# A new order for every engine's list in a two-branch kernel: warming matmuls, PSUM pairs and queues

## The chip, the cores and the metric

The kernel runs on one core of a Trainium2 chip. The metric is the device time of one execution in microseconds (us). TensorE is called PE here, VectorE DVE, ScalarE ACT, GpSimd POOL and SyncE SP, as the profile does. PE writes its results to PSUM, eight banks which this kernel uses as four pairs; ACT (and in four places DVE) takes them from there into SBUF, which is called an eviction. DMA transfers are issued from the queues of SP, ACT and POOL.

## The reference

Two branches work on the same input `x = A_q` (2048 rows, 640 columns) and are mixed by a gate per row.

```python
def _A_ref(q, k, v, shift_k, ssm_k, ssm_D):
    # k_shift: a causal convolution of k with 4 taps per column
    kv = k_shift * v
    # y: a long causal convolution of kv with ssm_k, by FFT of length 2 S
    y = y + kv * ssm_D
    return q * y

def _B_ref(x, w1, w2, w3, w4):
    h = _gelu(_layernorm(x) @ w1)
    # four groups of 160 columns of h, moved by +1, -1, +2, -2 rows
    hs = jnp.concatenate([g0, g1, g2, g3], axis=-1) @ w2
    x1 = x + hs
    return x1 + _gelu(_layernorm(x1) @ w3) @ w4

g = _sigmoid((x * gate_w).sum(-1, keepdims=True))
return g * a + (1 - g) * b
```

## The kernel before, in words

A row number is split as row = 1024 c + 8 p + rho: c is 0 or 1, p is one of the 128 partitions and rho one of 0 to 7. A step on a pair of rho is one of four stages sc.

**Branch B.** DVE takes the statistics of each rho (`bn`, L776 and L778; those of rho 1 are made on ACT, `st`), POOL raises the variance to the power -1/2 (`ln`, L756; this one instruction is called a power below), DVE normalizes (`xn`, L554), PE transposes through PSUM (`xTp`, L821, ten transpositions for one rho; rho 6 and 7 go by DMA, `xTd`, L818) and ACT evicts (`xTe`, L580). Then come the first matmul (`mm1`, L861, with Gelu in the eviction; for rho 0 and 1 in two halves `0a` and `0b`). The last 32 columns of each group come out in a matmul of their own (`gelu1t` is its eviction) and are moved to their places by small DMAs on POOL's queue (`tail`, L901). The second matmul (`mm2`, L971) starts from PSUM pairs that ACT has filled with x (`seed2`, L953). ACT makes the sums and the squares of the second normalization (`x1`, `sq`), and DVE and POOL finish it (`ln`, L794, L800 and L756), ACT normalizes rho 2 to 7 (`xn`, L566), SP transposes by DMA (`xT`, L998), and `mm3` (L1062) and `mm4` (L1033) follow.

**Branch A.** DVE forms kv from the four taps (`kv`, `kvb`, L549). The long convolution is done as a transform by matmuls with cosines and sines (`fwd`, L1091: `fwdh` for the taps of ssm_k, `fwdk` for kv), products on DVE with some of the sums done by accumulating DMAs on POOL's queue (`bh`, `bk`, `pw`, `fold`, L549 and L1121), and an inverse transform (`inv`, L1234). The taps reach SBUF by transpositions on PE for the first 320 columns (`tap`, L711), and by DMA for the others. POOL adds ssm_D to one row of the taps (`ssmD`, L721); the four `fwdh` jobs of the residue that holds this row wait for that.

**What sets the order.** The program first makes a list of 981 nodes (one engine's operation, a block of matmuls, or a DMA) with all their dependences. The class `Prog` then takes two lists that are written out in the source: `RANK` has a number for each node, and each engine works its nodes off in falling order of it; `PAIR` names the PSUM pair of each job of PE. A job waits until the evictions of the last job on its pair are done. `schedule` sorts and adds these dependences, `assign_waits` leaves out the waits that others already imply, and `emit` writes the engines' instruction streams. There is no other planning: an engine whose next node is not ready stands still. The numbers say nothing of times.

**Warming matmuls.** 96 nodes `fill` (L645) are matmuls of ones by ones, 128 columns wide, whose result nobody reads. They stand in `RANK` like the others; those that come behind PE's last useful node are dropped.

```python
    for i in range(FILL):
        P.stage = i * 8 // FILL
        P.pe([(lambda e, ps: e.matmul(bank(ps, 0, 128), ones, ones, start=True, stop=True)) for _ in range(FILLN)], r=[ones],
             cols=128 * FILLN, tag="fill", bits=(False, None))
```

Other small work ahead of and between the first transpositions: `gwt` (L651, five matmuls of one column), `shk` (L656, four times two matmuls that spread the taps over the partitions), `gsum` (L909), `halo` (L667), `gate` (L918).

Of the kernel before, what the change touches and what calls it, by code (L numbers as in the profile page):

```python
# [292 lines left out]
def _bf16_bits(a):  # L293
# [34 lines left out]
R4M = {("h",1),("k",1)}  # L328
FILL = 96
RANK = [  # L330
# [46 lines left out]
]  # L377
PAIR = [
# [7 lines left out]
]  # L386

def _freq(kap):
# [962 lines left out]
```

## Time and profile before

| what | before |
|---|---|
| time, three runs | 222.86, 223.73, 224.98 us; median 223.73 |
| the profiled execution | 226.48 us, span 224.4 us |
| PE busy | 216.7 us, 1520 matmuls, 81 of them warming ones |
| DVE, ACT, POOL busy | 205.3, 171.3, 62.0 us |
| mean granted clock of PE | 0.985 |
| moved by DMA | 39.76 MB |

The span runs from the first to the last instruction of the profiled execution; 226.48 - 224.4 = 2.1 us lie around it. A row of the timeline reads: start, length, engine and line, shapes, number of instructions, and in brackets the idle time ahead of it and who ended it. Matmuls overlap: the length of a row includes the time in which the last one leaves the array, so that the pace is read from one start to the next.

### The profile page before, as it was taken

To read this page: it belongs to the slowest core of one execution; us is meant where nothing else is said; L and a number is where in the kernel's file an instruction comes from. 1 tells how busy PE (TensorE), PEld (TensorE's weight loads), DVE (VectorE), ACT (ScalarE), POOL (GpSimd) and SP (SyncE) were. 2 spreads that over 40 slices of the span, in tenths; PEclk is the share of its full clock that TensorE was granted. 3 is DMA by queue.
4 is the path that set the end of the run, shared out by engine and by line. 5 is a ranking of instruction groups with operands and counts; after the bars stand their busy time and mean duration, and the time that the engine had idled before them with its cause. 6 is when DMAs were issued, how large, how long until landed. Compare 5 with 4: busy or idle time off the path is not lost.

```text
span 224.4 us, 3910 instructions
## 1 busy us (share of the span) xinstructions
PE 216.7 (97%) x1520; PEld 136.3 (61%) x1520; DVE 205.3 (91%) x307; ACT 171.3 (76%) x291; POOL 62.0 (28%) x64
## 2 busy tenths in 40 slices
PE   7899999799999999999999999999999999999993
PEld 7567766545767655446774554457764477666772
DVE  3896999999997999999998999999999989998764
ACT  4767998779999999999999998666423565396480
POOL 1232439255101302190062110222332303237000
PEclk9859999999999999999999999999999999999999
DMA  7999986759965640995443191087997975779768
GB/s 203 365 401 395 403 339 138 191 100 171 304 164 172 226 88 0 317 183 187 94 84 62 27 164 17 0 117 142 182 225 125 225 160 93 141 178 141 110 197 259
DMA packets 41579, 39.76 MB, mean 177 GB/s; under 512 B 20452, under 2 KB 34791, under 8 KB 41432
## 3 DMA queue, kind: packets, MB, share of 16 engines
q1 hardware_dynamic: 33864, 24.75, 38.3%
q0 software_dynamic: 7408, 14.42, 32.0%
q10 hardware_dynamic: 288, 0.33, 0.5%
q8 instruction: 12, 0.20, 0.4%
q14 instruction: 7, 0.06, 0.1%
HBM read 21.60 MB, written 3.93 MB: 114 GB/s over the span
## 4 chain that ended last, share of the span: by engine, by line
PE 66%; ACT 25%; POOL 3%; DMA 2%; DVE 1%; SPq 1%; issue 0%
PE PS L1033 23%; PE PS L1062 16%; ACT arena L580 16%; PE PS L861 8%; PE PS L1234 7%; PE PS L1091 6%; ACT arena L566 5%; ACT PS L953 4%; DMA arena<-in_A_q_dram 2%; POOL arena L901 2%; PE PS L821 2%; PE PS L711 1%; POOL arena L721 1%; PE PS L656 1%; PE PS L667 1%; SPq L592 1%
## 5 line engine op out<-in xcount | busy, mean ns | idle before, releaser
L549 DVE TENSOR_TENSOR arena<-arena 128x1280 bf16<-128x1280 bf16 (+5 forms) x212 | 182.3, 923 | 6.8 <-ACT arena L580 4.6
L580 ACT ACTIVATE arena<-PS 128x640 bf16<-128x640 f32 (+7 forms) x140 | 104.8, 814 | 22.9 <-PE PS L1062 8.0
L1033 PE MATMUL PS<-arena 128*128 128x320 bf16 x384 | 54.4, 299 | 0.5 <-ACT arena L580 0.5
L1062 PE MATMUL PS<-arena 128*128 128x512 bf16 x240 | 54.3, 379 | 0.0
L1033 PEld LDWEIGHTS PS<-arena 128*128 128x128 bf16 x384 | 37.5, 98 | 15.5 <-issue 0.8
L1121 POOL DMA_DIRECT2D arena<-arena x24 | 24.0, 1107 | 71.1 <-DVE arena L549 66.5
L580 ACT ACTIVATE arena<-PS,arena 128x320 bf16<-128x320 f32 (+1 forms) x48 | 26.5, 603 | 21.2 <-PE PS L1033 15.2
L1062 PEld LDWEIGHTS PS<-arena 128*128 128x128 bf16 x240 | 23.0, 98 | 26.8 <-ACT arena L580 1.2
L1091 PE MATMUL PS<-arena 128*128 128x320 bf16 x208 | 33.3, 300 | 1.7 <-POOL arena L721 1.3
L566 ACT ACTIVATE arena<-arena 128x640 bf16<-128x640 bf16 (+2 forms) x34 | 28.5, 865 | 2.0 <-DMA arena<-in_A_q_dram 1.8
L1091 PEld LDWEIGHTS PS<-arena 128*128 128x128 bf16 x208 | 19.0, 98 | 12.9 <-ACT arena L580 3.0
L756 POOL TENSOR_TENSOR arena<-arena 128x4 f32<-128x4 f32 (+1 forms) x9 | 18.7, 2077 | 27.4 <-DVE arena L554 23.9
L861 PE MATMUL PS<-arena 128*128 128x512 bf16 (+1 forms) x125 | 24.4, 353 | 0.0
L953 ACT ACTIVATE PS<-arena 128x640 f32<-128x640 bf16 x32 | 23.5, 744 | 0.3
L971 PE MATMUL PS<-arena 128*128 128x320 bf16 x160 | 22.9, 299 | 0.0
L971 PEld LDWEIGHTS PS<-arena 128*128 128x128 bf16 x160 | 15.2, 98 | 6.8 <-ACT PS L953 0.6
L861 PEld LDWEIGHTS PS<-arena 128*128 128x128 bf16 x125 | 12.7, 104 | 9.6 <-issue 0.5
L1234 PE MATMUL PS<-arena 128*128 128x320 bf16 x112 | 17.0, 299 | 0.0
L776 DVE BATCH_NORM_STATS2 arena<-arena 128x6 f32<-128x320 bf16 x28 | 12.1, 477 | 3.4 <-DMA arena<-in_A_q_dram 3.4
L901 POOL DMA_DIRECT2D arena<-arena x18 | 9.7, 544 | 16.2 <-ACT arena L580 16.2
L1234 PEld LDWEIGHTS PS<-arena 128*128 128x128 bf16 x112 | 10.7, 98 | 5.1 <-ACT arena L580 0.4
L645 PE MATMUL PS<-arena 128*128 128x128 bf16 x81 | 10.5, 277 | 1.2 <-DVE arena L602 1.2
(39 smaller groups left out, 72.8 us busy)
## 6 DMA issues: line engine op xcount, KB each, us to landing
arena<-arena POOLq DMA_DIRECT2D x18, 320.0 KB, 4.6
arena<-in_B_w_dram POOLq DMA_DIRECT2D x4, 960.0 KB, 6.3
arena<-in_A_k_dram SPq DMA_DIRECT2D x4, 640.0 KB, 9.7
arena<-in_A_v_dram SPq DMA_DIRECT2D x4, 640.0 KB, 16.4
arena<-arena POOLq DMA_DIRECT2D x4, 640.0 KB, 6.1
arena<-in_A_q_dram SPq DMA_DIRECT2D x4, 640.0 KB, 7.3
out_dram<-arena SPq DMA_DIRECT2D x15, 160.0 KB, 2.1
arena<-in_A_q_dram SPq DMA_DIRECT2D x6, 320.0 KB, 5.5
```

What stands on the lines that cost most here:

```text
L549: return dve(lambda e: e.tensor_tensor(o, a, b, op), [a, b], [o], c_tt(n), tag=tag, **kw)
L566: node = P.op("act", lambda e, ps: e.activation(o, i, func, **kw), r=r, w=[o], cost=c_act(n, naps, acc is not None, psum=False), tag=tag, ...
L580: node = P.op("act", lambda e, ps: e.activation(ov, inner(ps), func, **kw), r=r, w=[o], cost=c_act(n, len(r), acc is not None), job=job, t ...
L756: P.op("pool", lambda e, ps: e.tensor_tensor(r, v, hv, ALU.pow), r=[v, HALF], w=[r], cost=cost, tag="ln")
L861: fns.append(lambda e, ps, b=b, c=c, lhsT=lhsT: e.matmul(bank(ps, b, 256 * n), lhsT, XT[:, c, r0:r0 + n, :], start=(c == 0), stop=(c == 4)))
L953: P.seed(job, lambda e, ps: e.activation(two(ps, 320), x, ACTF.Copy), [X[:, c, rho, :]], c_act(640, psum=False), tag)
L971: fns.append(lambda e, ps, hh=hh, ft=ft, lhsT=lhsT: e.matmul(bank(ps, hh, 320), lhsT, w2v[:, ft, 320 * hh:320 * hh + 320], start=False, st ...
L1033: fns.append(lambda e, ps, hh=hh, ft=ft, lhsT=lhsT: e.matmul(bank(ps, hh, 320), lhsT, w4h[ft // 6][:, ft % 6, 320 * hh:320 * hh + 320], st ...
L1062: fns.append(lambda e, ps, b=b, ft=ft, c=c, sc=sc: e.matmul(bank(ps, b, 512), w3h[ft // 6][:, c, 128 * (ft % 6):128 * (ft % 6) + 128], XT[ ...
L1091: fns.append(lambda e, ps, w=w, b=b, rhs=rhs, st=(first and n == 0), en=(n == len(ss) - 1): e.matmul(bank(ps, b, 320), w, rhs, start=st, s ...
L1121: return P.dma("pool", lambda e, ps: e.dma_start(o, i, accum_op=ALU.add, max_dma_last_dim=2560), r=[o, i], w=[o], nbytes=nb, cost=1.2, kin ...
L1234: fns.append(lambda e, ps, w=w, z=z, c=c, st=(n == 0), en=(n == len(terms) - 1): e.matmul(bank(ps, c, 320), w, z[:, c, :], start=st, stop=en))
```

## The change

`RANK` and `PAIR` get other numbers; nothing else in the source is touched. No operation is added, removed or changed in size, but for the warming matmuls: 94 of the 96 are now ahead of PE's last useful node, where 81 were.

```diff
 FILL = 96
 RANK = [
-    977, 925, 973, 972, 980, 975, 962, 957, 952, 938, 933, 915, 926, 976, 940, 967, 834, 881, 849, 946, 827,
...
+    978, 977, 965, 972, 980, 964, 959, 949, 954, 924, 907, 916, 877, 973, 930, 971, 802, 873, 793, 936, 783,
...
 PAIR = [
-    1, 0, 2, 2, 3, 1, 2, 2, 1, 1, 3, 1, 1, 1, 1, 3, 2, 3, 0, 3, 0, 3, 3, 1, 0, 0, 1, 2, 0, 2, 1, 1, 3, 2, 2, 3,
...
+    0, 3, 0, 1, 0, 1, 0, 3, 2, 1, 3, 3, 2, 0, 2, 1, 0, 2, 2, 1, 3, 3, 3, 2, 1, 0, 0, 2, 2, 0, 0, 3, 1, 1, 0, 0,
...
```

The numbers can be read only once the nodes are sorted by them. These are the stretches of the lists where the two orders differ most (the number behind a name is the rho or the stage; `fill x24` is 24 warming matmuls).

```
PE before   fill x24, gwt, fill x26, shk, fill x4, gsum, fill x6, xTp:0, shk, fill x2, shk, halo:1, halo:0,
            xTp:1, mm1:0a, mm1:0a, shk, mm1:0b, mm1:0a, mm1:0b, xTp:2, fill, xTp:3, mm1:0b, tap x3, mm1:1, ...
            behind xTp:0 21 more fill: two, then ones, and once five in a row
PE after    fill x63, shk, fill x27, gwt, fill, xTp:0, fill x2, shk, fill, gsum, shk, halo:1, xTp:1, mm1:0a,
            mm1:0a, shk, mm1:0b, xTp:3, halo:0, mm1:0b, xTp:2, tap, mm1:0a, xTp:4, mm1:1, mm1:0b, tap, ...
            behind xTp:0 3 more fill
POOL before ident, ln:0, ln:1, w1t, ln:2, tail:0, ln:4, ln:6, tail x8, ssmD, tail x7, w3:0, tail x2, ssmD,
            w3:1, ln (stage 0), w4:1, w4:0, pwTa, pwSa, GM, ln, ln, ln (stages 1 to 3), pwTa, pwSa, ...
POOL after  ident, ln:0, ln:1, ln:2, w1t, tail x2, ln:4, tail, ln:6, tail x6, ssmD, tail x9, ssmD, w3:0, w3:1,
            ln (stage 0), GM, w4:1, w4:0, ln (stage 1), pwTa, pwSa, ln, ln (stages 2, 3), pwTa, pwSa, ...
SP before   gate_w, x:1, shift_k, x:1, x:3 x2, k:1, w1, x:5 x2, x:7 x2, ssm x3, k:0, D x2, FM:0, w2 x2, v:0,
            FM:1, v:3, v:2, k:3, v:1, kh, w2 x3, xTd x4, w2, k:2, w2 x2, tT ...
SP after    D, shift_k, x:1 x2, x:3 x2, gate_w, k:1, w1, x:5, x:7, x:5, w2, ssm, x:7, k:0, ssm, FM:1, w2 x2, ssm,
            w2, kh, w2 x3, FM:0, v:0, v:2, k:3, v:1, w2, xTd x4, D, k:2, v:3, tT ...
```

On DVE the first normalization `xn:0` moves ahead of a statistics block that waits for the second column block's load, and between the statistics `ln:4` and `xn:4` stand five `bn` operations, where two `xn` and five `bn` stood. ACT's list has the eviction of `gwt` ahead of the first `shk` in both orders, while on PE `gwt` now comes 27 warming matmuls behind that `shk`. On ACT two of the four `xn:5` move ahead of the second `seed4`, and one square of stage 3 moves behind them. PE's last eighteen blocks, from the job ahead of the first `inv` of the second half, have the same pattern in both orders.

102 rows, old and new, of tables (PAIR, RANK) are left out of this document.

## The prediction

> **What bounds the kernel now.** I read the page first, then the chain of waits, then busy times by stretches, and last the timelines of the head.
>
> ```profile
> span 224.4 us, 3910 instructions
> PE 216.7 (97%) x1520; PEld 136.3 (61%) x1520; DVE 205.3 (91%) x307; ACT 171.3 (76%) x291; POOL 62.0 (28%) x64
> PEclk9859999999999999999999999999999999999999
> PE 66%; ACT 25%; POOL 3%; DMA 2%; DVE 1%; SPq 1%; issue 0%
> ```
>
> PE is busy for 97% and carries 66% of the chain that ended last, and DVE with 91% has nearly as little room. The fourth digit of the clock row is a 5: early on the clock was halved for a slice. Two lines of the chain of waits and two stretches (busy PE, PEld, DVE, ACT, POOL, then the clock) tell the rest:
>
> ```profile
> 53.34 1.04 ACT arena L580
> 101.89 6.68 PE PS L1033 x48
> 53.00:101.00 48.00, 47.78 (x346) 29.42 (x345) 45.48 (x59) 47.54 (x103) 13.94 (x13) 1.00 0.67 178
> 101.00:221.00 120.00, 119.01 (x764) 73.48 (x761) 112.97 (x163) 82.21 (x128) 27.76 (x24) 1.00 0.66 130
> ```
>
> From 53.3 to 101.9 us the chain runs over ACT's evictions, and PE is busy for 47.78 of 48 us beside it; from there to the end it is PE alone, 119.01 of 120 us. Behind 53 us an order of the lists can win little: PE's idle time there is 0.2 + 1.0 us, DVE's 2.5 + 7. What can be won lies ahead of 53 us. What can be lost lies anywhere, since three engines are nearly full.
>
> **The clock in the head.** First the clock by half microseconds (the clock is the column ahead of the last two), then PE's timeline.
>
> ```profile
> 9.50:10.00 0.50, 0.50 (x6) 0.12 (x3) 0.50 (x2) 0.27 (x1) 0.00 (x0) 1.00 1.08 381
> 10.00:10.50 0.50, 0.50 (x4) 0.13 (x2) 0.47 (x4) 0.50 (x1) 0.08 (x1) 0.51 1.03 384
> 16.50:17.00 0.50, 0.50 (x5) 0.39 (x4) 0.50 (x3) 0.50 (x2) 0.00 (x0) 0.67 0.96 385
> 1.18 2.74 PE L645 MATMUL PS<-arena 128*128 128x128 bf16 x24 [1.18 <-DVE arena L602]
> 4.07 2.81 PE L645 MATMUL PS<-arena 128*128 128x128 bf16 x26
> 6.81 0.72 PE L656 MATMUL PS<-arena 1*128 1x320 bf16 x2
> 7.83 0.49 PE L645 MATMUL PS<-arena 128*128 128x128 bf16 x6
> 8.97 0.72 PE L821 MATMUL PS<-arena 128*128 128x128 bf16 x10 [0.65 <-DVE arena L778]
> 11.26 1.78 PE L667 MATMUL PS<-arena 128*128 128x480 bf16 x4
> 12.83 1.27 PE L821 MATMUL PS<-arena 128*128 128x128 bf16 x10
> 13.90 3.78 PE L861 MATMUL PS<-arena 128*128 128x256 bf16 x20
> 17.61 0.72 PE L656 MATMUL PS<-arena 1*128 1x320 bf16 x2
> 18.27 2.36 PE L861 MATMUL PS<-arena 128*128 128x256 bf16 x20
> 20.46 0.72 PE L821 MATMUL PS<-arena 128*128 128x128 bf16 x10
> 21.02 0.22 PE L645 MATMUL PS<-arena 128*128 128x128 bf16 x1
> ```
>
> The clock is 1.00 up to 10.0 us, 0.50 from there to 16.7. The warming matmuls show that it was also low at the start, which the page does not record: the 26 of the second row take (6.81 - 4.07) / 26 = 0.105 us each, the six of 7.83 only (0.49 - 0.22) / 5 = 0.054. So PE is slow until about 6.6 us, then fast, then slow again from 10.0 to 16.7. What the second slow stretch costs is read from equal work at full clock: twenty matmuls of 256 columns take 17.61 - 13.90 = 3.71 us in it and 20.46 - 18.27 = 2.19 behind it (1.52 lost); ten transpositions 13.90 - 12.83 = 1.07 against 21.02 - 20.46 = 0.56 (0.51 lost); four of 480 columns 1.57, at half that 0.78 lost. Together 2.8 us, all on PE's path.
>
> Between 6.8 and 10.0 us PE has little dense work: ten warming matmuls, single-row jobs, ten transpositions and 0.65 us of idle time. The new order has 63 + 27 + 1 = 91 warming matmuls ahead of the first transposition, where 24 + 26 + 4 + 6 = 60 stood, and they run on without a hole to the transposition. I take it that the clock then holds: PE's thin stretch shrinks to the time between the first transposition and the first mm1, some 3.3 us with a halo job in it, against 6.8 to 13.9 before. Gain 2.8, bounds 0 and 2.8.
>
> The Trainium skill ("TensorE: Matmul & The Clock Gate", the table "Why this matters for your kernels") asks only for no idle gaps of more than about 3 us. By that rule the 0.65 us could not have halved the clock, the warming matmuls would buy nothing, and the sum would be 2.8 us poorer. The rows disagree: the clock fell at 10.0 us with no gap of that size.
>
> **What the warming matmuls cost.** Fifty run at the slow pace up to 6.8 us, or 6.6 without the gwt job among them. The other 40 ahead of gwt take 40 x 0.054 = 2.2, the shk pair 18.27 - 17.61 = 0.66, gwt about 0.2: the first transposition starts at 9.7 instead of 8.97, 0.75 later. Its input is there by then (it was the wait that ended at 8.97, and xn:0 moves up on DVE). Bounds: nothing if the clock rises a microsecond sooner, 1.3 if it rises so much later. Behind the first transposition 3 warming matmuls stand instead of 81 - 60 = 21: 18 x 0.054 = 1.0 less, of which gsum, which moves behind it, takes 0.1 back: -0.9. Where these stood in waits they cost nothing, so the gain is 0 to 0.9; I keep 0.9, as PE's idle rows are few.
>
> **POOL's small transfers.**
>
> ```profile
> 29.29 3.40 PE L861 MATMUL PS<-arena 128*128 128x512 bf16 x15
> 20.26 0.61 POOL L901 DMA_DIRECT2D arena<-arena  x1 [5.62 <-ACT arena L580]
> 20.90 1.04 POOL L756 TENSOR_TENSOR arena<-arena 128x4 f32<-128x4 f32 x1
> 32.99 4.28 POOL L901 DMA_DIRECT2D arena<-arena  x8 [3.68 <-ACT arena L580]
> 37.29 3.11 POOL L721 TENSOR_TENSOR arena<-arena 1x320 bf16<-1x320 bf16 x1
> 38.53 0.64 PE L918 MATMUL PS<-arena 128*128 128x1 bf16 x20
> 40.46 3.16 PE L1091 MATMUL PS<-arena 128*128 128x320 bf16 x22 [1.29 <-POOL arena L721]
> ```
>
> Eight transfers, held by an eviction of ACT (gelu1t of the second row pair), and the addition of ssm_D behind them keep PE idle for 1.29 us. The new list leaves six between the power ln:6 and the addition: 2 x 4.28 / 8 = 1.1 less. Against that, the five matmuls whose eviction they wait for now follow both blocks of ten of their stage, one block (2.2 us) later than before. ACT has the same evictions ahead of it in both lists. PE being 2.8 - 0.75 = 2.0 ahead, its five (the first of the 15 in the first row, at 0.216 each: 29.29 + 1.1 = 30.4 before) end at 30.4 - 2.0 + 2.2 = 30.6, the eviction by some 31.4 (32.7 before, when ACT came to it late), the transfers by 31.7 + 3.2 = 34.9, the addition by 38.0. Counted at the paces of the rows, PE's list has 27.2 us of work from the first transposition to the waiting job, where 26.85 stood, so PE comes to it at 39.17 - 2.0 + 0.35 = 37.5. The wait shrinks from 1.3 to 0.5: -0.8, bounds -1.3 and +1 (an addition is 3.11 or, by the page's mean of two, less).
>
> **DVE and the end.**
>
> ```profile
> 22.05 0.80 DVE L554 TENSOR_SCALAR arena<-arena 128x640 bf16<-128x640 bf16 x2 [1.86 <-POOL arena L756]
> 71.06 0.16 DVE L794 SCALAR_TENSOR_TENSOR arena<-arena 128x4 f32<-128x4 f32 x1 [1.52 <-ACT arena L580]
> 197.83 4.01 DVE L549 TENSOR_TENSOR arena<-arena 128x1280 bf16<-128x1280 bf16 x5
> 202.63 1.25 PE L1234 MATMUL PS<-arena 128*128 128x320 bf16 x8
> ```
>
> The last fold ends at 201.84 and PE's first inverse job of the second half starts at 202.63: if DVE came no sooner, PE could gain only 0.8 us. So DVE must give some 2.7 to 3 too. Its 1.86 wait is for the power of 20.90, which had stood behind the transfer of 20.26 since that waited 5.62 us for ACT. In the new order two transfers stand ahead of the power, but ACT evicts both halves of gelu1t early; with PE's earlier mm1 they go by 17 to 18 us and the power is there in time. The 1.52 wait is for ACT's squares and shrinks with ACT. Together up to 3.4 us, bounds 0.5 and 3.4. SP's queue costs nothing: k:2 and v:3 now stand behind the four transpositions xTd, but the tap transpositions behind them wait for all loads in both orders, and the product with v:3 comes only behind the row of 71.06; gate_w is needed only by a gwt that is later.
>
> **The sum.** On PE: -2.8 + 0.75 - 0.9 - 0.8 = -3.75; DVE allows -0.8 - 3.4 = -4.2 at best. The other moves (pairs, evictions, products) I take at nothing, bounds -1 and +1 by the 1.2 us of idle time that PE has behind 53. I take -3.5: span 220.9, and the profiled execution 226.48 - 3.5 = 223.0. The median of the runs stands 2.75 below the profiled execution, and the runs differ by 2.1 us. Part of this may be the clock stretch, which a run need not have in full. I count half of it, 1.4, as missing in the median: 223.73 - (3.5 - 1.4) = 221.6, with 220.4 to 222.8 as this case's own range.
>
> **The rivals.** The median has the clock stretch in full: 223.73 - 3.5 = 220.2. For it: the thin stretch from 6.8 to 13.9 us is in every run.
>
> The median does not have it at all: 223.73 - (3.5 - 2.8) = 223.0. For it: the 2.75 us between profile and median are the 2.8 of the clock; against it: the three runs spread over 2.1. The Trainium skill (the same page, Part 1) says that the activity window runs free of the kernel's start, so that such a stretch may fall differently from run to run; no run here shows the clock without a profile.
>
> The clock falls in the new order too, in the thin stretch from 9.7 to 13 us, and halves mm1 and the transpositions as in the rows above: 221.6 + 2.8 = 224.4 at worst. DVE does not come sooner and the end stays where it is but for 0.8: 223.73 - 0.8 = 222.9. Then the change doesn't do on DVE what it does on PE.
>
> Slower: ACT stands still at the first xn:5, which now stands ahead of the second seed4 and the evictions of the transforms.
>
> ```profile
> L953 ACT ACTIVATE PS<-arena 128x640 f32<-128x640 bf16 x32 | 23.5, 744 | 0.3
> 103.34 2.77 ACT L566 ACTIVATE arena<-arena 128x640 bf16<-128x640 bf16 x3
> 99.36 0.16 DVE L800 SCALAR_TENSOR_TENSOR arena<-arena 128x4 f32<-128x4 f32 x1
> 96.58 2.75 POOL L756 TENSOR_TENSOR arena<-arena 128x4 f32<-128x4 f32 x1
> 113.94 5.12 POOL L756 TENSOR_TENSOR arena<-arena 128x4 f32<-128x4 f32 x1 [12.54 <-DVE arena L554]
> ```
>
> Its input is ready at 99.5, 0.2 us behind POOL's power of 2.75 us; ACT came to it at 103.3. By its new place (a square, a seed and two evictions fewer ahead, four operations at up to the 23.5 / 32 = 0.73 us of a seed: some 2.5 us) and the gain of 3.5 ACT comes at 97.3. If DVE is no sooner, it waits 2.2 us, and if the power takes 5.12 as the row of 113.94, 2.4 more: 4.6. ACT's evictions are the chain there, so that 221.6 + 4.6 = 226.2; it turns slower than before from a wait of 2.1 us. Against it: the first mm4 block can cover 3 us of it on PE.
>
> **How the numbers follow.** Forecast 221.6: 0.44. Clock stretch in full 220.2: 0.18; none of it 223.0: 0.15; the clock falls again 224.4: 0.08; ACT at xn:5 226.2: 0.11; DVE no sooner 222.9: 0.04. One per cent, which is about what can be told from no change, is 2.2 us: faster means below 221.5, slower above 226.0. Half of the forecast's case (0.22) and the full stretch make 0.40 faster; 0.07 of the xn:5 case and 0.01 of the falling clock make 0.08 slower; 0.52 stays. The range from 219.6 to 224.8 leaves out some 0.07 below and 0.09 above.
>
> **What would show it.** Right: no half of the clock between 10 and 17 us, twenty matmuls of 256 columns in 2.2 us, the first transposition near 9.7, POOL's addition near 38 and PE's wait for it under 1 us, DVE's wait at xn:4 gone, the last fold near 198.5. Wrong: a 5 in the clock row, DVE's last fold still at 201, or ACT idle ahead of L566 near 97.

## The result: 1.2% slower

The changed kernel takes 227.03 us (median of six runs, 226.62 to 227.32), the kernel before beside it 224.81 (six runs, 222.86 to 226.75). The ratio is 1.0119, with a 95% interval from 1.0074 to 1.0163. The profiled execution of the changed kernel took 226.62 us, with a span of 224.8. The forecast was 221.6, so it missed the sign.

The page of the changed kernel, the lines that answer those shown of before (13 matmul records are missing in this trace, so PE's busy time is a little low):

```profile
span 224.8 us, 3937 instructions
...
PE 214.0 (95%) x1520; PEld 134.6 (60%) x1533; DVE 206.1 (92%) x307; ACT 171.6 (76%) x291; POOL 70.1 (31%) x64
...
PEclk9999999999999999999999999999999999999999
...
PE 44%; DVE 23%; ACT 16%; POOL 10%; DMA 4%; issue 2%; SPq 0%; ACTq 0%; DVEq 0%
```

The 5 in the clock row is gone, as forecast. But the chain has changed hands: PE had 66% of it, POOL 3% and DVE 1%; now they have 44, 10 and 23. POOL is busy for 8.1 us more with the same work. The chain of waits in order of time shows where (start, length, who):

```profile
50.23 1.04 ACT arena L580
...
74.45 4.85 ACT arena L580 x9
...
79.33 1.57 DVE arena L549 x2
...
88.67 8.14 POOL arena L756
96.81 3.77 DMA arena<-arena
...
103.95 3.69 POOL arena L756
...
117.55 4.40 POOL arena L756
```

The first row stood at 53.34 before: up to there the new order is 3.1 us ahead. At 79.33 the chain passes to DVE's products, and then come three powers of POOL and one DMA; the chain of before has no power in it. The stretches, kernel before first, then the changed one (busy PE, PEld, DVE, ACT, POOL):

```profile
80.00:112.00 32.00, 31.37 (x193) 18.00 (x192) 31.54 (x49) 32.00 (x59) 7.71 (x7) 1.00 0.56 147
```

```profile
80.00:112.00 32.00, 29.55 (x179) 17.08 (x180) 26.60 (x43) 29.81 (x54) 15.29 (x6) 1.00 0.57 146
```

DVE stands still for 32 - 26.60 = 5.4 us here, where it stood 0.5. Its timeline, and below it POOL's:

```profile
88.42 0.16 DVE L554 TENSOR_SCALAR arena<-arena 128x4 f32<-128x4 f32 x1
88.49 7.52 DVE L549 TENSOR_TENSOR arena<-arena 128x1280 bf16<-128x1280 bf16 x11
96.87 0.16 DVE L800 SCALAR_TENSOR_TENSOR arena<-arena 128x4 f32<-128x4 f32 x1 [0.86 <-POOL arena L756]
100.61 0.90 DVE L549 TENSOR_TENSOR arena<-arena 128x1280 bf16<-128x1280 bf16 x2 [3.57 <-DMA arena<-arena]
...
107.66 0.17 DVE L800 SCALAR_TENSOR_TENSOR arena<-arena 128x4 f32<-128x4 f32 x1 [0.93 <-POOL arena L756]
```

```profile
88.67 8.17 POOL L756 TENSOR_TENSOR arena<-arena 128x4 f32<-128x4 f32 x1 [2.38 <-DVE arena L554]
96.81 1.80 POOL L1121 DMA_DIRECT2D arena<-arena  x2
103.95 3.68 POOL L756 TENSOR_TENSOR arena<-arena 128x4 f32<-128x4 f32 x1 [5.34 <-DVE arena L554]
117.55 4.39 POOL L756 TENSOR_TENSOR arena<-arena 128x4 f32<-128x4 f32 x1 [9.93 <-DVE arena L554]
```

The same stretch in the kernel before: first POOL's two transfers ahead of its power of 96.58, then DVE's operations beside that power (three products and one of 128x4 in the first row, 3 x 0.74 + 0.16 = 2.4 us):

```profile
94.84 1.81 POOL L1121 DMA_DIRECT2D arena<-arena  x2 [4.69 <-DVE arena L794]
...
96.07 2.37 DVE L549 TENSOR_TENSOR arena<-arena 128x1280 bf16<-128x1280 bf16 x4
98.36 0.17 DVE L554 TENSOR_SCALAR arena<-arena 128x16 f32<-128x16 f32 x1
```

The reader is to see four things. The power of stage 1 takes 8.17 us; before, at 96.58, it took 2.75. It ends at 96.84, 0.8 us behind the end of DVE's run of L549 (88.49 + 7.52 = 96.01: ten products of 128x1280 and a last one of 128x4), and DVE waits 0.86 for it at L800. The accumulating transfers `pwTa` and `pwSa` (L1121), which stood ahead of the power before (94.84) and now stand behind it, are issued at 96.81 only. And DVE, whose new list needs the landing of pwTa for its next product (`pwTy`), stands for another 3.57.

### The profile page after: what moved, and what is told of

It reads as the page before. It is cut to its first block, busy times and chain, and to the rows that moved or that the text cites. A ratio compares the mean times of both kernels' runs of the same rounds, so it can differ in the third digit from the quotient of the medians.

```text
span 224.8 us, 3937 instructions
## 1 busy us (share of the span) xinstructions
PE 214.0 (95%) x1520; PEld 134.6 (60%) x1533; DVE 206.1 (92%) x307; ACT 171.6 (76%) x291; POOL 70.1 (31%) x64
## 4 chain that ended last, share of the span: by engine, by line
PE 44%; DVE 23%; ACT 16%; POOL 10%; DMA 4%; issue 2%; SPq 0%; ACTq 0%; DVEq 0%
DVE arena L549 18%; PE PS L1033 15%; PE PS L1062 11%; ACT arena L580 9%; POOL arena L756 7%; PE PS L861 7%; PE PS L1234 6%; ACT PS L953 3%; ACT arena L566 3%; DVE arena L776 3%; PE PS L1091 3%; DMA arena<-in_A_q_dram 2%; DMA arena<-arena 2%; POOL arena L901 1%; POOL arena L721 1%
## 5 line engine op out<-in xcount | busy, mean ns | idle before, releaser
L549 DVE TENSOR_TENSOR arena<-arena 128x1280 bf16<-128x1280 bf16 (+5 forms) x212 | 182.9, 925 | 8.2 <-DMA arena<-arena 3.6
L580 ACT ACTIVATE arena<-PS 128x640 bf16<-128x640 f32 (+7 forms) x140 | 102.8, 795 | 21.1 <-PE PS L1062 9.6
L1062 PE MATMUL PS<-arena 128*128 128x512 bf16 x230 | 53.1, 379 | 0.8 <-issue 0.2
L1121 POOL DMA_DIRECT2D arena<-arena x24 | 23.9, 1063 | 63.7 <-DVE arena L549 58.7
L756 POOL TENSOR_TENSOR arena<-arena 128x4 f32<-128x4 f32 (+1 forms) x9 | 24.6, 2734 | 29.8 <-DVE arena L554 26.5
L566 ACT ACTIVATE arena<-arena 128x640 bf16<-128x640 bf16 (+2 forms) x34 | 25.9, 783 | 5.2 <-DMA arena<-in_A_q_dram 2.8
L953 ACT ACTIVATE PS<-arena 128x640 f32<-128x640 bf16 x32 | 22.7, 723 | 0.3
L861 PE MATMUL PS<-arena 128*128 128x512 bf16 (+1 forms) x122 | 22.6, 335 | 0.2
L554 DVE TENSOR_SCALAR arena<-arena 128x640 bf16<-128x640 bf16 (+3 forms) x31 | 9.7, 335 | 1.0 <-POOL arena L756 0.9
```

The source lines that it names most:

```text
L549: return dve(lambda e: e.tensor_tensor(o, a, b, op), [a, b], [o], c_tt(n), tag=tag, **kw)
L566: node = P.op("act", lambda e, ps: e.activation(o, i, func, **kw), r=r, w=[o], cost=c_act(n, naps, acc is not None, psum=False), tag=tag, ...
L580: node = P.op("act", lambda e, ps: e.activation(ov, inner(ps), func, **kw), r=r, w=[o], cost=c_act(n, len(r), acc is not None), job=job, t ...
L756: P.op("pool", lambda e, ps: e.tensor_tensor(r, v, hv, ALU.pow), r=[v, HALF], w=[r], cost=cost, tag="ln")
L861: fns.append(lambda e, ps, b=b, c=c, lhsT=lhsT: e.matmul(bank(ps, b, 256 * n), lhsT, XT[:, c, r0:r0 + n, :], start=(c == 0), stop=(c == 4)))
L953: P.seed(job, lambda e, ps: e.activation(two(ps, 320), x, ACTF.Copy), [X[:, c, rho, :]], c_act(640, psum=False), tag)
```

## The experiments

Theory A said that the place of one power on POOL's queue, together with DVE's reordered products, makes the whole loss; theory B that the loss comes from the rest of the new order or from the warming. Each number below is a median with its runs' range, and its ratio, with a 95% interval, is to the kernel before on the same chip. Most edits are lines put in behind the two lists, so that line numbers shift by a few; the remarks behind `#` are added here.

**One transfer ahead of the power.**

```diff
+RANK[638] = RANK[401] + 0.5     # pwTa of stage 0 ahead of POOL's power of stage 1
```

> The changed kernel with one accumulating DMA of the first product (pwTa of stage 0) ahead of the power of stage 1 on POOL, and nothing else moved. Theory A: in the changed kernel that power takes 8.2 us beside DVE's products, the DMA is issued only behind it, DVE waits 3.6 us for its landing, and everything behind 100 us follows DVE. Then the 3.6 us wait is gone here, and the time falls by 2.5 to 3.6 us, to 223.4 to 224.5. Theory B: the loss is PE's own new order and its PSUM pairs behind 53 us. Then DVE's wait goes too, but the time stays within 1 us of 227.0.

223.04 us (222.68 to 223.22), ratio 0.9911 [0.9882, 0.9940]. POOL's timeline in it:

```profile
89.96 0.94 POOL L1123 DMA_DIRECT2D arena<-arena  x1 [3.33 <-DVE arena L551]
90.58 6.61 POOL L758 TENSOR_TENSOR arena<-arena 128x4 f32<-128x4 f32 x1
97.16 0.86 POOL L1123 DMA_DIRECT2D arena<-arena  x1
```

The power still takes 6.61 us, but pwTa is issued at 89.96, DVE's wait of 3.57 is gone, and the time falls by 4.0 us against the changed kernel, a little more than the 2.5 to 3.6 expected: one number among 981 turns 1.2% slower into 0.9% faster.

**The power behind both transfers**, as before:

```diff
+RANK[401] = RANK[648] - 0.5     # POOL's power of stage 1 behind pwTa and pwSa
```

> The changed kernel with the power of stage 1 behind both accumulating DMAs of the first product on POOL, as the kernel before had it. Theory A: DVE's wait of 3.6 us is gone as in the run with one DMA ahead, but the power starts some 6 us later, near 95, and ACT may wait 1 to 2 us for the first xn:5 in its place: 223.5 to 226. Theory B: within 1 us of 227.0.

222.93 us (222.59 to 223.40), ratio 0.9921 [0.9891, 0.9952]. The same as the last, and below the 223.5 to 226 expected:

```profile
94.27 2.96 POOL L758 TENSOR_TENSOR arena<-arena 128x4 f32<-128x4 f32 x1
```

The power starts 3.7 us later than in the last kernel, but ends at the same time (94.27 + 2.96 = 97.23, beside 90.58 + 6.61 = 97.19), so that ACT sees no difference.

**Less warming in the new order.**

```diff
+for i in (120, 42, 106, ...):   # 31 warming matmuls fewer, 60 left ahead of xTp:0
+    RANK[i] = -1
```

> The changed kernel with 60 warming matmuls ahead of the first transposition, as before, 31 fewer than it has. Theory A with the clock: the clock falls to 0.50 for some 6.8 us again in most runs, the head gives back 1 to 2.8 us less the 1.7 us of the shorter start; DVE still waits behind the power near 100; time 226.5 to 228.5 with a spread of over 1 us. Rival: the warming matmuls are themselves the loss, and the time falls by 1.7 us to 225.3.

227.45 us (226.91 to 227.92), ratio 1.0115 [1.0072, 1.0157]. The clock does fall without them (granted clock from 11 to 14 and from 14 to 17 us, the last but two column), but the power still takes its 8.17:

```profile
11.00:14.00 3.00, 2.46 (x17) 1.95 (x17) 3.00 (x11) 1.71 (x3) 1.69 (x2) 0.61 1.06 390
14.00:17.00 3.00, 3.00 (x21) 1.83 (x19) 2.94 (x12) 2.33 (x5) 0.00 (x0) 0.82 1.03 403
```

So the warming is not what costs. Fewer warming matmuls and the fallen clock together make no difference that can be measured (ratio 1.0115 beside 1.0119): by 88 us DVE is late by no more than 0.54 (the power starts at 89.21 instead of 88.67), and behind that the chain runs over DVE and POOL.

**More warming in the order before.**

```diff
+for i in (136, 109, 134, ...):  # 31 more warming matmuls ahead of xTp:0
+    RANK[i], PAIR[i - 42] = 870.5, 1
```

> The kernel before with 31 more warming matmuls right ahead of its first transposition (91 in all, as in the changed kernel), all else in its old order. Clock theory: the granted clock holds at 1.00 behind 6.6 us, the 2.8 us of the slow stretch are gone, 0.7 us are paid at the start, the time is 222.5 to 223.5 in every run, that is at the lower end of the runs of the kernel before, with a spread below 1 us. Rival: the clock stretch doesn't set the spread of the runs of before, and the time is 0.7 us above their median, 225.5.

224.26 us (223.88 to 226.19), ratio 0.9993 [0.9961, 1.0026]: no gain that can be measured, and a miss for what was expected. The profiled execution (225.83 us, mean granted clock 0.991) has its clock by stretches:

```profile
10.00:17.00 7.00, 7.00 (x61) 4.46 (x59) 7.00 (x27) 6.21 (x8) 2.44 (x3) 1.00 1.05 400
38.00:39.50 1.50, 1.02 (x5) 0.67 (x6) 1.50 (x2) 0.00 (x0) 0.42 (x1) 0.74 0.72 144
39.50:42.70 3.20, 3.20 (x16) 1.89 (x14) 3.13 (x4) 2.12 (x3) 0.00 (x0) 0.59 0.87 254
```

The clock holds from 10 to 17 us, and then falls from about 38.7 to 42.1 (1.5 x 0.26 / 0.5 = 0.8 us of the second stretch at half, 3.2 x 0.41 / 0.5 = 2.6 of the third) at the next thin place: the one-column gate matmuls and PE's wait for POOL's addition of ssm_D, now 1.52 us. The 22 forward matmuls behind the wait take 4.84 us there instead of 3.16.

This second fall doesn't explain the median, though. Three of the twelve runs have a mean clock of 0.991 and take 225.68 to 226.19 us; the other nine have 0.998 to 1.000 and take 223.88 to 224.61, median 224.23. With the clock held, the old order gains some 0.6 us on 224.81, where 222.5 to 223.5 was expected. The 31 matmuls more are 31 x 0.054 = 1.7 us of PE at its fast pace (an estimate, at the 0.054 us each that the prediction read); whether they take the rest was not tried.

**The same, and warming in that wait too.**

```diff
...
+for i in (122, 137, 92, 128, 108):   # five nodes of four warming matmuls each, ahead of the waiting job
+    RANK[i], PAIR[i - 42] = 710, 2
...
```

> The order before with 31 more warming matmuls ahead of the first transposition, as in the earlier run of that kind, and 20 more (five nodes of four each) on PE directly ahead of the fwdh job that waits for POOL's addition of ssm_D near 38 us; no useful operation is moved. Theory A (the gain of the held clock in the head was given back at 39.5 to 42.7 us, where the clock fell once more beside that wait): the clock stays at 1.00 from 7 us on, 22 forward matmuls at 38.5 take 3.2 instead of 4.84 us, the eviction chain behind mm1 starts 2 us sooner than the 53.3 of before, and the time is 1.5 to 2.5 us under the kernel before, if DVE's end comes sooner too; Theory B (DVE sets the end in the old order whatever PE gains in the head): the clock holds, but the last fold ends at 201 and the time is within 0.8 us of the kernel before.

223.83 us (223.48 to 224.82), ratio 0.9955 [0.9930, 0.9980]. The clock stays up (0.998 to 1.000 in all twelve runs), the forward matmuls take 3.16 again, and the chain's first eviction behind mm1 starts at 51.58 instead of 53.34:

```profile
36.65 1.28 PE L651 MATMUL PS<-arena 128*128 128x128 bf16 x20
38.71 3.16 PE L1097 MATMUL PS<-arena 128*128 128x320 bf16 x22 [0.78 <-POOL arena L727]
```

Of the 1.8 us gained there, 1.1 show in the medians (224.94 beside it). That lies between the two theories (1.5 to 2.5, or under 0.8), and 0.4 below the nine runs with a held clock above, on another chip.

**The power ahead of the transfers in the order before.**

```diff
+RANK[638], RANK[648] = RANK[401] - 0.3, RANK[401] - 0.6
```

> The order before, with the two accumulating transfers of stage 0 (pwTa, pwSa) moved behind POOL's power of stage 1, as in the new order, and nothing else. Theory A (the loss comes from the power ahead of the transfers together with DVE's new order, which needs their landing some 6 us sooner than the old one): the power of stage 1 becomes longer than 2.75 us, the transfers are issued 2 to 4 us later than 94.8, DVE's first product that needs them stands only at 103 us, and the time is 0 to 0.7 us over that of the kernel before (ratio 1.000 to 1.003). Theory B (the place of the power alone costs it): a DVE wait of 2 us or more for the landing, ratio 1.009 or more.

224.27 us (222.55 to 226.21), ratio 0.9981 [0.9944, 1.0018]. The same place of the power costs nothing in the old order. The power did not become longer, as was expected, but shorter: 1.56 us. In the old DVE list the first product behind the statistics is followed by a 128x4 operation, and by its new start, some 0.6 us ahead of that one, the power comes out behind it.

```profile
94.51 1.56 POOL L759 TENSOR_TENSOR arena<-arena 128x4 f32<-128x4 f32 x1 [5.55 <-DVE arena L557]
```

In the kernel before, the power started only 0.2 us ahead of the same operation and ended 1 us behind the start of the next short one, that of 98.36. So this run doesn't try a long power in the old order: the transfers behind it are issued at 96.03, only 1.2 us later than before.

**DVE stands still for the power.**

```diff
+RANK[402] = RANK[401] - 0.5     # DVE's L800, which waits for the power, ahead of the products
```

> The new order, with one number changed: DVE's operation L800 of stage 1, which waits for POOL's power of stage 1, is put directly behind the statistics that feed the power, ahead of the eleven products that ran beside it. POOL's list is that of the new order: the power still stands ahead of pwTa and pwSa. Theory A (the power gets on only while DVE runs no products): DVE stands still for about 1 us, the power takes 1.0 to 1.2 us instead of 8.17, pwTa is issued near 90 instead of 96.8, DVE's wait of 3.57 for its landing is gone, and the time is 222.7 to 224.0. Theory B (the power is slow in this stretch for another reason, such as the queue or the DMA traffic): the power still takes over 3 us, DVE stands for as long in front of it, and the time is 226 to 230.

223.38 us (222.73 to 224.14), ratio 0.9945 [0.9920, 0.9970]. POOL's list is untouched, and yet:

```profile
88.73 1.54 POOL L759 TENSOR_TENSOR arena<-arena 128x4 f32<-128x4 f32 x1 [2.38 <-DVE arena L557]
90.25 0.91 POOL L1124 DMA_DIRECT2D arena<-arena  x1
```

The power takes 1.54 instead of 8.17 because DVE stops behind one product, and the time lies in the range expected by the theory that the power waits for DVE (222.7 to 224.0). What makes it long is DVE's run of products.

**Does DVE have to stand, or is a break enough?** Two kernels add small operations on DVE behind the first product that follows the statistics of stages 1, 2 and 3, and move nothing.

```diff
...
+    for _ in range(3):
+        ts(DUM, HALF, 1.0, None, ALU.mult, None, 4, tag="brk")     # 128x8 f32, into a scratch tile
+    P.schedule(RANK + [466.5, 420.0, 369.0], PAIR)
```

> The new order with three small operations added on DVE and nothing moved: a tensor_scalar of 128x8 f32 into a scratch tile, one behind the first product that follows the statistics of each of the stages 1, 2 and 3, so that DVE's run of back-to-back two-input products is broken once, while POOL's power of that stage is waiting in it. Theory A1 (the power gets in at the first operation of DVE that is not a large two-input product, and then ends 0.9 us later beside the next product): the power of stage 1 takes 1.5 to 2 us instead of 8.17, those of stages 2 and 3 under 2.6 instead of 3.68 and 4.39; DVE's three waits of 0.9 at L800 and its 3.57 for pwTa's landing are gone; 220.5 to 222.5 us. Theory A2 (it needs DVE to stand still for 0.9 us): the power still takes 8.2, the four waits stay, 226.6 to 227.6 us.

222.75 us (222.49 to 223.09), ratio 0.9896 [0.9877, 0.9915], the lowest median of this study, though 0.25 us above the 220.5 to 222.5 expected. DVE's timeline, then POOL's:

```profile
88.44 0.82 DVE L550 TENSOR_TENSOR arena<-arena 128x1280 bf16<-128x1280 bf16 x1
89.17 0.17 DVE L555 TENSOR_SCALAR arena<-arena 128x8 f32<-128x8 f32 x1
89.26 6.77 DVE L550 TENSOR_TENSOR arena<-arena 128x1280 bf16<-128x1280 bf16 x10
95.95 0.15 DVE L801 SCALAR_TENSOR_TENSOR arena<-arena 128x4 f32<-128x4 f32 x1
```

```profile
88.61 1.55 POOL L757 TENSOR_TENSOR arena<-arena 128x4 f32<-128x4 f32 x1 [2.37 <-DVE arena L555]
90.14 0.91 POOL L1122 DMA_DIRECT2D arena<-arena  x1
...
99.35 2.22 POOL L757 TENSOR_TENSOR arena<-arena 128x4 f32<-128x4 f32 x1 [5.18 <-DVE arena L555]
112.35 1.51 POOL L757 TENSOR_TENSOR arena<-arena 128x4 f32<-128x4 f32 x1 [10.78 <-DVE arena L555]
```

One operation of 0.17 us lets the power in, which then ends beside the next products; these are no slower for it ((6.77 - 0.16) / 9 = 0.73 us from one to the next, against (7.52 - 0.16) / 10 = 0.74, with 0.16 for the 128x4 one). DVE's three waits of 0.9 and the one of 3.57 are gone. Yet the interval overlaps that of the kernel with one transfer moved: with DVE out of the way, ACT's evictions and PE make up the chain of waits again, as before the change:

```profile
74.40 6.04 ACT arena L581 x11
...
99.08 6.52 PE PS L1034 x48
```

With two `bn_stats` of 128 columns in each place instead:

```diff
+    for _ in range(6):
+        dve(lambda e: e.bn_stats(DUM[:, 0:6], ones), [ones], [DUM], 0.2, tag="brk")
...
```

> The same with two bn_stats of 128 columns (one input, a 128x6 f32 output into a scratch tile) in each of the three places instead of the tensor_scalar, some 0.4 us of DVE in each: a longer break made of the form beside which the power of stage 0 to 3 of the first normalization took 1.05 us at 18.18. Theory A1: as in the run with the tensor_scalar, 0.3 to 0.8 us dearer, 221 to 223 us. Theory A2: the power gets on during the break only, 0.4 us of the 0.9 that it needs; it still takes over 7 us, 227 to 228.5 us.

223.43 us (222.69 to 223.74), ratio 0.9923 [0.9899, 0.9946]; powers of 1.54, 2.21 and 1.51. The same effect, the time 0.4 us above the range expected; the longer break is not needed.

## Why the prediction was wrong, point by point

**The head came out as worked out.** No half of the clock between 10 and 17 us; the first transposition at 9.45 (9.7 forecast), POOL's addition ended at 37.80 (38.0), PE's wait for it 0.54 (0.5), DVE's waits of 1.86 and 1.52 gone (a new one of 0.93 at 27.09, for a power of 3.53 beside a product of 2.82, was not forecast). PE's timeline of the changed kernel:

```profile
9.45 0.72 PE L821 MATMUL PS<-arena 128*128 128x128 bf16 x10
...
12.76 1.80 PE L861 MATMUL PS<-arena 128*128 128x256 bf16 x15
14.49 0.72 PE L656 MATMUL PS<-arena 1*128 1x320 bf16 x2
...
37.86 2.35 PE L1091 MATMUL PS<-arena 128*128 128x320 bf16 x16 [0.54 <-POOL arena L721]
```

Fifteen matmuls of 256 columns take 14.49 - 12.76 = 1.73, or 2.3 for twenty (2.2 forecast). The sum of the head, -3.75 on PE, shows as -3.1 at the first eviction of the chain.

**The step that failed** is "the other moves (pairs, evictions, products) I take at nothing, bounds -1 and +1". It bounded the loss by PE's 1.2 us of idle time in the old order, which says what PE could gain, not what it could lose. Two moves in it cost 4.0 us together (the run with one transfer moved): the power of stage 1 ahead of pwTa on POOL, and DVE's new list, which puts ten unbroken products beside that power and pwTy, which needs pwTa, right behind it. The first alone, in the old DVE order, costs nothing (ratio 0.9981 [0.9944, 1.0018]), for there the power stays short. With that fault taken out, the new order gives 222.9 to 223.0, about 1.9 us under the 224.81 beside it, against the -2.1 forecast for the median. That this comes so near doesn't show each part of the sum, and the time itself would still be 1.3 us above the 221.6, as the three runs that it started from lay low.

**The rows were there.** The prediction quoted the powers of 2.75 and 5.12 and let them be long for ACT's `xn:5`. It didn't ask why one instruction takes 1.04, 2.75 and 5.12 us. In the trace of the kernel before, DVE's wait for the one of 5.12, which ends at 119.06, looks like the new one at 96.87:

```profile
119.10 0.17 DVE L800 SCALAR_TENSOR_TENSOR arena<-arena 128x4 f32<-128x4 f32 x1 [0.90 <-POOL arena L756]
```

With "a power ends when DVE's products do", DVE's new run of ten products behind the statistics would have given an end of some 96 us and a pwTa behind it. The rival for slower had the right instruction and the wrong waiter: ACT's first `xn:5` starts at 97.92 without a wait; the loss sits on DVE, through the DMA queued behind the power. That its 226.2 lies near the measured 227.03 is chance.

The Trainium skill ("SBUF — State Buffer", "Who interferes with whom") states that a DVE instruction with two SBUF inputs contends with a GpSimd instruction that reads SBUF, and that issue order decides which of the two fully blocks. The rows of 8.17 and 1.54 agree that one blocks, and go further: POOL stayed out through ten products, not one.

**The other rivals.** The clock did not fall again (mean 0.999 to 1.000 in all six runs). "DVE no sooner" came true at the end, but through the waits between 88 and 122 us and not because DVE kept its old pace.

**The end of DVE's last fold**, forecast near 198.5, came at 193.47 + 9.46 = 202.93:

```profile
193.47 9.46 DVE L549 TENSOR_TENSOR arena<-arena 128x1280 bf16<-128x1280 bf16 x12
```

That is 1.1 us later than before; the first inverse job of the second half starts at 203.56 instead of 202.63. In the kernel with one transfer moved it starts at 200.25.

**Half of the clock stretch in the median.** Each run comes with its mean granted clock, so this can be read. Of 64 later runs of the kernel before one had 0.985, as the profiled one, 40 had 0.990 to 0.992 (median 225.2 us) and 23 had 0.996 to 1.000 (median 224.4). Halved for 6.7 us, the clock's mean over 224 us is 1 - 3.35/224 = 0.985; 0.991 is 2.0 us lost. So most runs have somewhat more than half of the stretch, if it lies in the head as in the profiled one, and the assumption held. The profiled execution of the old order with the power ahead of the transfers, with a mean of 0.992, shows such a half in the head: its granted clock from 10 to 17 us is 0.76, that is 7.0 x 0.24 / 0.5 = 3.4 us at half, as long as the stretch from 38.7 to 42.1 above. But the three runs that the forecast started from, median 223.73, lay lower than the later ones. Four of the 64 runs had 1.000 and took 222.6 to 223.6 us, close to the 222.9 to 223.0 of the new order without its fault. This suggests that most of the new order's gain is the clock's; it isn't shown, for the old order with more warming held its clock too and took 223.48 us or more.

## What to carry to other kernels

Read the durations of one instruction across the whole trace: where a 128x4 operation takes 1 us here and 8 us there, find what its neighbour engine does in each, before any list is reordered. A transfer that another engine waits for belongs ahead of such an operation on its queue, and a small operation between DVE's long runs of products can let POOL in, as it did in all six places tried here. And look at every thin place of PE: a clock that was held at 10 us fell at 39 in the profiled run with more warming.

## What the runs showed of the hardware

POOL's power of 128x4 takes 1.05 us beside DVE's bn_stats (and 1.04 at 20.90 in the kernel before, while DVE stood still) and up to 8.17 beside a run of ten two-input products, ending 0.8 to 0.9 us behind the end of the run in the changed kernel's rows at 88.67 and 103.95. The first is shown by these rows of DVE and of POOL in the changed kernel:

```profile
17.79 2.06 DVE L776 BATCH_NORM_STATS2 arena<-arena 128x6 f32<-128x320 bf16 x5
```

```profile
18.18 1.05 POOL L756 TENSOR_TENSOR arena<-arena 128x4 f32<-128x4 f32 x1
```

A 0.17 us tensor_scalar between two products cuts the 8.17 to 1.55. What in the break lets it in stays open: in the kernel before the power of 99.89 ended after 1.51 us beside products without a small operation between them, and the one of 96.58 did not get in at a 128x4 operation that came 0.2 us behind its start. Lengths on POOL are rough in such a profile, but DVE's waits at L800 and the times at which POOL issues its next transfer say the same.

The clock fell with some 1.5 us of idle time or less at two places: at 10.0 us in the kernel before (0.65 idle, small matmuls), and near 38.7 in the profiled run of the old order with more warming (1.52 idle beside one-column matmuls). At the latter job it did not fall in the changed kernel with 0.54 idle, nor in the kernel before with 1.29, and the mean clocks of the other runs with more warming (nine of twelve at 0.998 or more) say that it mostly held there too. What decides it stays open. The rule of the Trainium skill that the prediction weighed ("TensorE: Matmul & The Clock Gate", the table "Why this matters for your kernels") asks only that no idle gap be longer than about 3 us. Both falls came without such a gap, so keeping that rule was not enough here.
